# The last batch's first product as eight groups of seven block products, in another order of the tail

## The chip, the cores and the metric

The kernel runs on one core of a Trainium2 chip. The metric is the device time of one execution in microseconds (us); a kernel's time is the median of its runs. Of each kernel one execution was recorded by the hardware profiler; its engines are PE (TensorE, the matrix unit, whose results land in PSUM banks), DVE (VectorE), ACT (ScalarE), POOL (GpSimd) and SP (which issues DMAs).

## What is computed

Attention with normalised queries and keys, and behind it two matrix products with an activation between:

```python
q_n = q / (norm(q) + 1e-6);  k_n = k / (norm(k) + 1e-6)          # 8 batches, 12 heads, 448 x 64
attn = softmax(q_n @ k_n.T / tau);  x = (attn @ v)               # as 3584 tokens x 768
h = x @ w_in                                                     # 768 x 2048, the first product
g = h * clip(h + 3, 0, 6) / 6                                    # "hardswish"
out = g @ w_out                                                  # 2048 x 768, the second product
```

## The kernel before

**Stages.** A batch has 448 tokens and six pairs of heads. A plan written out by hand starts the kernel; then a loop takes one pair of heads after the other, and puts between the attention's steps matmul *units* of the two products of earlier batches. After the last pair, the *tail* has the units that are left: a part of the first product of batch 6, the whole first product of batch 7, and the second products of batches 5 to 7. The change lies in the tail alone, some 60 us.

**The order of the tail** is written out by hand in `LAST` (line 62), and read by `listed` (line 1034) into a list of units, `units[NP]` (lines 1109 to 1113). `do("UU", len(stream), "avp")` (line 1279) issues one unit after the other. A unit issues its matmuls and hangs steps that finish it on three lists, for ACT, DVE and POOL; after each unit the three lists are emptied in that order, and a step may hang a further step on a list. So the text of `LAST` sets the order of every engine's queue, and each engine works its queue strictly in order.

**Banks.** Six PSUM banks (four named M, and Y and Z) are taken in turn (`next_bank`, line 166) by whatever unit asks for a new one. A unit can start only when the last reader of what its bank held before is done.

**The first product, plain.** `mm1_unit` (line 581) makes 128 of the 2048 features for 448 tokens: 6 matmuls of 448 columns (L587), a relu on ACT (L596), and a product with a clip on DVE (L602). In the list these are `f14` (batch 6) and `F6` (batch 7).

**The first product, in seven block products.** `seven_unit` (line 920) makes two such units, n and n + 8, at once: both matrices are cut in 2 x 2 blocks, and seven products of sums of blocks (Strassen's way, Winograd's form of the numbers 1 to 7) give the four blocks of the result, with 3 matmuls of 224 columns for each, 21 in all (L947). A group is issued in four parts: `A2` is products 3 and 4 of group 2, `B2` is product 7, `C2` products 5 and 2, `D2` product 6; product 1 goes with A or B. The parts A and C share one bank, B and D another. The finishing steps of a group:

- after A, ACT copies the first results to SBUF (L1001, L1003), and POOL adds their halves (L1006). The letter of `M1_BY` says how product 1 gets in: with `p`, product 1 is issued with A and POOL adds it (L1008); with `v`, it is issued with B and DVE adds it later.
- after C, ACT makes the relu (L970) of two of the four result blocks, DVE makes the differences for the other two (L1014, or L1017 and L1019 where the letter is `v`) and the product with the clip for the first two (L973).
- after D, DVE makes the last sum (L1022); then ACT makes its relu (L984) and the clip and product follow. The letter of `H_BY` says where: `v` is DVE (L992), `p` is POOL.

The scratch for these (`trio`) has room for three groups. The seven products need sums of blocks of the weights (`w_sum_of`, L898, in the list `w7.2v`: product 7, groups 4 and 5, on DVE; part p serves groups 2p and 2p + 1) and of the activations (`x_sum_of`, L915, in the list `x4`). Before the change, groups 0 to 5 are made this way, and units 6, 7, 14 and 15 are plain.

**The second product** takes pairs of 128-token blocks, numbered 0 to 10, in the same seven products: `4.7` (`product_unit`, line 769, 8 matmuls of 384 columns, L788) is product 4 of pair 7. Pairs 9 and 10 are those of batch 7, so they need all sixteen units of the first product; product 4 reads the odd rows of g, product 3 the even ones. `g9:6` is the sum of blocks for product 6 of pair 9 (`g_sum`, L766). Products 3, 4, 5 and 2 are copied out by ACT (L836, L807), 1, 6 and 7 are added by DVE (L845, L813), and POOL makes three sums of a pair's parts (L817, L818, L821). `s6.1` (`single_unit`, line 859, 16 matmuls, L868) is a 128-token block of batch 6 that has no partner, and DVE copies it out (L878). `gl` copies a left-over part of g between batches (L578).

Of the kernel before, what the change touches and what calls it, by code (L numbers as in the profile page):

```python
# [59 lines left out]
]  # L60

LAST = [
# [3 lines left out]
]  # L66
H_BY, M1_BY = "vvvvvvpp", "pppvpppp"


@with_exitstack  # L70
def kernel(
# [543 lines left out]
    def result(b, t, cols, o, end=None):  # L615
        for e in range(2):
            if t < 3:
                r = out[b * S : (b + 1) * S].rearrange("(p c) m -> c p m", c=7)[2 * t + e + b % 2]
            else:
                r = out[(b - 1 + e) * S : (b + e) * S].rearrange("(p c) m -> c p m", c=7)[6 * (1 - e)]  # L620
            eng = nc.scalar if end is not None and e else nc.sync
            eng.dma_start(out=r[:, cols], in_=o[64 * e : 64 * e + 64, 0 : cols.stop - cols.start])
# [146 lines left out]
    def product_unit(n, name, end=None, apart=False):  # L769

        need = {"3": ["y3"], "4": ["y4"], "1": "1", "6": "6", "7": "7"}.get(name, [])
        assert all((x, c) in summed for x in need for c in range(KC))
        if name not in "34":
            assert (n, name) in g_summed
        base = None if apart else {"2": "4", "5": "3", "6": "1"}.get(name)
        if base is None:
            banks[n, name] = bank_of(None, 1)
        ps, key = banks.pop((n, base)) if base else banks[n, name]
        c0, width = (MH // 2 * end, MH // 2) if end in (0, 1) else (0, MH)
        if name in "167":  # L780
            lhs, rhs = sum_of(n, name), w_sum[name]
        else:
            i, k = {"3": (0, 0), "4": (1, 1), "2": (1, 0), "5": (0, 1)}[name]
            m = LEFT if name in "42" else RIGHT
            lhs, rhs = block(n, i, k), w_out_sb[:, :, m].rearrange("p (c k) m -> p c k m", k=2)[:, :, k, :]
        m = ps[:, c0 : c0 + width]
        for c in range(KC):
            nc.tensor.matmul(  # L788
                m,
                lhs[:, c, :],  # L790
                rhs[:, c, c0 : c0 + width],
                start=(base is None and c == 0),
                stop=(c == KC - 1),
                skip_group_check=True,
            )
        issued_products.add((n, name))
        d, e = d_and_e(n)
        if base is None and name in "34":
            unread[key] = 1 + ((n, name) not in APART)

        def done(i, o, cols):
            unread[key] = 0
            result(*PAIRS[n][i], cols, o, end)

        def copied(i, cols):
            o = out_tile()
            nc.scalar.copy(out=o[:, :], in_=m)  # L807
            parts[n, name] = o
            done(i, o, cols)

        def added(i, cols, x):
            parts[n, name] = o = out_tile()
            nc.vector.tensor_tensor(out=o[:, 0:width], in0=m, in1=x[:, c0 : c0 + width], op=ALU.add)  # L813
            done(i, o, slice(cols.start + c0, cols.start + c0 + width))

        def both():
            nc.gpsimd.tensor_tensor(out=e, in0=d, in1=e, op=ALU.add)  # L817
            nc.gpsimd.tensor_tensor(out=d, in0=e, in1=parts[n, "5"][:, :], op=ALU.subtract)  # L818

        def rest():  # L820
            nc.gpsimd.tensor_tensor(out=e, in0=e, in1=parts[n, "2"][:, :], op=ALU.subtract)  # L821

        def added_later(i, cols, x):
            parts[n, name] = o = out_tile()
            nc.scalar.copy(out=o[:, :], in_=m)
            unread[key] = 0

            def add():
                nc.gpsimd.tensor_tensor(out=o[:, :], in0=o[:, :], in1=x, op=ALU.add)
                result(*PAIRS[n][i], cols, o)  # L830

            post["p"].append(add)

        def finish():
            if name in "34":
                nc.scalar.copy(out={"3": d, "4": e}[name], in_=m)  # L836
                unread[key] -= 1
            elif apart:
                added_later(*{"5": (0, RIGHT, d), "2": (1, LEFT, e)}[name])
            elif name == "5":  # L840
                copied(0, RIGHT)
            elif name == "2":
                copied(1, LEFT)
            elif name == "1":
                nc.vector.tensor_tensor(out=d, in0=m, in1=d, op=ALU.add)  # L845
            elif name == "6":
                added(1, RIGHT, e)
            else:
                added(0, LEFT, d)
            ready.add((n, name))  # L850
            first = {(n, x) for x in ("245" if (n, "4") in APART else "45")}
            if (n, name) in first and first <= ready:
                post["p"].append(both)
            if name in "245" and {(n, "4"), (n, "5"), (n, "2")} <= ready:
                post["p"].append(rest)

        post["a" if name in "2345" else "v"].append(finish)

    def single_unit(b, m):

# [59 lines left out]
    def seven_unit(n, part):  # L920
# [39 lines left out]
        def g_out(first):  # L960
# [4 lines left out]
            step = (FCN // 2 * (S + SR) + (-HS if first else HS)) // 2  # L965
            return bass.AP(tensor=g.tensor, offset=g.offset, ap=[g.ap[0], [step, 2], [1, HS // 2]]).bitcast(BF16)

        def relu():
            u = sb.tile([128, S], BF16, name="u", tag="u", bufs=3)
            nc.scalar.activation(out=u[:, :], in_=ps[:, 0:S], func=AF.Relu, bias=half_bias, scale=1.0 / 6.0)  # L970

            def product():
                nc.vector.scalar_tensor_tensor(  # L973
                    out=g_out(1), in0=halves_of(u[:, :]), scalar=1.0, in1=halves_of(ps[:, 0:S]), op0=ALU.min, op1=ALU.mult
                )
                unread[key] = 0

            post["v"].append(product)

        def clipped():  # L980
            u = sb.tile([128, S], BF16, name="u", tag="u", bufs=3)
            e = H_BY[n]
            if e == "v":
                nc.scalar.activation(out=u[:, :], in_=h, func=AF.Relu, bias=half_bias, scale=1.0 / 6.0)  # L984
            else:
                nc.scalar.activation(out=s, in_=h, func=AF.Relu, bias=half_bias, scale=-1.0 / 6.0)
                nc.scalar.activation(out=u[:, :], in_=s, func=AF.Relu, bias=1.0, scale=-1.0)

            def product():
                o, x, y = g_out(0), halves_of(u[:, :]), halves_of(h)  # L990
                if e == "v":
                    nc.vector.scalar_tensor_tensor(out=o, in0=x, scalar=1.0, in1=y, op0=ALU.min, op1=ALU.mult)  # L992
                else:
                    nc.gpsimd.tensor_tensor(out=o, in0=x, in1=y, op=ALU.mult)
                g_done.update(((BL, n), (BL, n + FCN // 2)))
                seven_done.add(n)

            post[e].append(product)
# [11 lines left out]
            post["p"].append(added)  # L1010

        def differences():
            if M1_BY[n] == "p":
                nc.vector.tensor_tensor(out=h, in0=t, in1=ps[:, 0:S], op=ALU.subtract)  # L1014
                return
            same = t[:, HS:S].unsqueeze(1).to_broadcast([128, 2, HS])
            nc.vector.tensor_tensor(out=halves_of(h), in0=same, in1=halves_of(ps[:, 0:S]), op=ALU.subtract)  # L1017
            m1 = seven[n]["B"][0][:, HS:S]
            nc.vector.tensor_tensor(out=h[:, 0:HS], in0=m1, in1=h[:, 0:HS], op=ALU.add)  # L1019
# [40 lines left out]
    def products(text):  # L1060

        u = []
        for x in text.split():
            name, n = x.split(".")
            if name[0] == "s":
                u.append((single_unit, int(name[1]), int(n)))
            else:
                u.append((product_unit, int(n), name[0], None, name[1:] == "a"))
        return u
# [37 lines left out]

    assert len(carry) == 2
    units[NP] = [x for line in LAST for x in listed(line)]
    units[NP] += products("3.9 4.9") + sums(9, "1") + products("5.9") + sums(10, "75") + products("2.9 3.10") + sums(10, "62")  # L1110
    units[NP] += products("4.10 5.10") + sums(10, "1") + products("2.10 1.9 1.10")
    units[NP] += [(product_unit, n, x, 2) for n, x in ((9, "7"), (9, "6"), (10, "6"))]
    units[NP] += [(product_unit, 10, "7", x) for x in range(2)]

# [200 lines left out]
```

## Time and profile before

| | us |
|---|---|
| runs | 403.27, 403.36, 404.13 (median 403.36) |
| the profiled execution's own time | 403.54 |
| its span, first to last instruction | 401.7 |
| TensorE busy | 392.0 |
| tail: 4.7 starts | 339.1 |
| tail: the first group starts | 349.2 |
| tail: the first product of pairs 9 and 10 starts | 379.4 |

A row of the profile's timeline reads: start and length in us, engine, line, operation, what is written from what is read, partitions x elements and types, count; in brackets, how long the engine stood idle before and whom it waited for. Matmul lengths overlap, so the price of a piece is the step from its start to the next one's. PEld is the loading of weights into TensorE. The chain is the row of work that ended last, followed back. A tile's name is that of its memory: `at`, `nrm`, `tT`, `xT` and `gT` are reused in the tail, so that `big<-w_in_sb` or `nrm<-w_in_sb` is a weight sum, `at<-xT` a sum of activations, and `gT<-...` with f32 the scratch of a group.

### The profile page before, as it was taken

How to read it: one execution, taken by the hardware profiler on the slowest of the kernel's cores; microseconds unless marked ns; L12 is line 12 of the kernel's file. 1: busy time of each engine (PE TensorE's matmuls, PEld its weight loads, DVE VectorE, ACT ScalarE, POOL GpSimd, SP SyncE). 2: the span in 40 equal slices, each digit the busy share in tenths (PEclk: the TensorE clock that was granted, in tenths of full speed). 3: DMA queues.
4: the chain of work that ended last, by engine and by line, in shares of the span. 5: the costliest groups of instructions: out<-in, count | busy, mean ns of one | idle time of the engine just before them, and what ended most of it. 6: DMA issues, size and time to landing. Idle time of an engine off the chain costs nothing.

```text
span 401.7 us, 9814 instructions
## 1 busy us (share of the span) xinstructions
PE 392.0 (98%) x3743; PEld 239.4 (60%) x3743; DVE 300.9 (75%) x535; ACT 280.2 (70%) x615; POOL 262.8 (65%) x253
## 2 busy tenths in 40 slices
PE   7988999999999999999999999999999999999996
PEld 5656556555665556655555556556555556687563
DVE  7998787877588777777857887587656676888863
ACT  5999989887377687787768768768758755265330
POOL 6899936753644996598486875776674893344270
PEclk9999999999999999999999999999999999999999
DMA  8999999698868658686779748966763522130133
GB/s 288 317 237 227 200 226 250 137 202 191 194 156 200 146 115 223 172 214 137 182 192 203 166 117 164 180 187 140 187 154 80 111 47 55 34 79 21 39 81 97
DMA packets 93166, 63.75 MB, mean 159 GB/s; under 512 B 56128, under 2 KB 93120, under 8 KB 93120
## 3 DMA queue, kind: packets, MB, share of 16 engines
q1 hardware_dynamic: 87408, 56.45, 59.6%
q0 software_dynamic: 5312, 6.29, 9.6%
q8 instruction: 29, 0.48, 0.5%
q10 hardware_dynamic: 400, 0.39, 0.3%
q14 instruction: 17, 0.14, 0.1%
HBM read 45.61 MB, written 11.01 MB: 141 GB/s over the span
## 4 chain that ended last, share of the span: by engine, by line
PE 91%; ACT 4%; DVE 4%; issue 1%; ACTq 0%; DVEq 0%
PE M L587 21%; PE M L788 16%; PE PV L482 11%; PE Z L587 6%; PE M L442 6%; PE Y L587 5%; PE Z L788 5%; PE Y L788 5%; PE M L868 4%; PE M L634 3%; ACT at L460 2%; PE PV L1136 2%; PE M L947 2%; PE Y L442 1%; PE Z L442 1%; DVE n L248 1%
## 5 line engine op out<-in xcount | busy, mean ns | idle before, releaser
L460 ACT ACTIVATE at<-M 128x448 bf16<-128x448 f32 x194 | 96.6, 562 | 23.2 <-PE M L442 20.6
L587 PE MATMUL M<-xT,w_in_sb 128*128 128x448 bf16 x462 | 99.2, 352 | 0.2
L587 PEld LDWEIGHTS <-w_in_sb 128*128 128x128 bf16 x696 | 65.3, 98 | 56.8 <-issue 2.8
L293 POOL TENSOR_TENSOR nrm<-big,r 128x896 bf16<-128x896 f32 (+1 forms) x47 | 78.7, 1679 | 15.4 <-issue 5.5
L236 POOL TENSOR_TENSOR big<-big 128x896 f32<-128x896 f32 (+5 forms) x45 | 68.5, 1528 | 12.9 <-DVE gT L602 8.3
L482 PEld LDWEIGHTS <-at 128*128 128x128 bf16 (+1 forms) x1536 | 54.1, 97 | 19.9 <-issue 12.1
L602 DVE SCALAR_TENSOR_TENSOR gT<-u,M 128x448 bf16<-128x448 bf16 x73 | 44.6, 618 | 28.5 <-ACT u L596 27.8
L482 PE MATMUL PV<-vx,at 128*128 128x65 bf16 (+1 forms) x1536 | 62.7, 193 | 0.0
L596 ACT ACTIVATE u<-M,bias 128x448 bf16<-128x448 f32 x77 | 50.2, 656 | 15.1 <-PE M L587 14.7
L399 POOL COPY km<-tT 64x128 bf16<-64x128 bf16 x34 | 14.4, 423 | 60.8 <-DMA tT<-nrm 26.3
L248 DVE TENSOR_REDUCE n<-big 128x14 f32<-128x896 f32 (+1 forms) x50 | 51.6, 1038 | 0.3 <-ACT big L234 0.2
L788 PEld LDWEIGHTS <-gT 128*128 128x128 bf16 x288 | 27.8, 98 | 19.0 <-DVE gT L766 0.2
L788 PE MATMUL M<-w_out_sb,gT 128*128 128x384 bf16 x192 | 35.0, 326 | 0.0
L503 DVE TENSOR_TENSOR on<-PV,rc 128x512 bf16<-128x512 f32 x48 | 33.2, 692 | 1.7
L442 PE MATMUL M<-tT,kz 64*128 64x448 bf16 (+1 forms) x171 | 30.9, 351 | 0.5 <-ACT at L460 0.5
L460 ACT ACTIVATE at<-Y 128x448 bf16<-128x448 f32 x50 | 28.1, 562 | 4.3 <-PE Z L442 4.3
L788 PEld LDWEIGHTS <-gs 128*128 128x128 bf16 x224 | 21.5, 98 | 14.7 <-DVE gs L766 0.4
L312 POOL CAST vx<-big 128x512 bf16<-128x512 f32 x39 | 28.3, 730 | 2.9 <-DMA big<-in_v_dram 2.8
L460 ACT ACTIVATE at<-Z 128x448 bf16<-128x448 f32 x50 | 28.1, 563 | 2.6 <-PE M L442 2.6
L587 PE MATMUL Z<-xT,w_in_sb 128*128 128x448 bf16 x120 | 26.0, 353 | 0.0
L587 PE MATMUL Y<-xT,w_in_sb 128*128 128x448 bf16 x114 | 24.7, 352 | 0.0
L766 DVE TENSOR_TENSOR gs<-gT 128x1024 bf16<-128x1024 bf16 x26 | 23.5, 904 | 0.0
(165 smaller groups left out, 641.4 us busy)
## 6 DMA issues: line engine op xcount, KB each, us to landing
big<-in_k_dram SPq DMA_DIRECT2D x24, 448.0 KB, 4.9
big<-in_q_dram SPq DMA_DIRECT2D x24, 448.0 KB, 4.3
out_dram<-o SPq DMA_DIRECT2D x107, 96.0 KB, 2.2
big<-in_v_dram SPq DMA_DIRECT2D x48, 128.0 KB, 4.6
big<-in_v_dram SPq DMA_DIRECT2D x48, 96.0 KB, 4.5
w_in_sb<-in_moe_w_in_dram POOLq DMA_DIRECT2D x8, 384.0 KB, 9.1
w_out_sb<-in_moe_w_out_dram POOLq DMA_DIRECT2D x4, 768.0 KB, 10.6
tT<-nrm SPq DMA_TRANSPOSE x34, 2.8
```

Source lines behind the costliest of these rows:

```text
L236: engines[e].tensor_tensor(out=o, in0=i, in1=i, op=ALU.mult)
L248: nc.vector.tensor_reduce(out=n2_and_r[0][:, d % 2, j % 2, c], in_=sq[:, :, :, :].rearrange("p g c d -> p (g c) d")[:, c, :], axis=AX.X, o ...
L293: engines[e].tensor_tensor(out=nrm[:, :, g, :].rearrange("p c g d -> p g c d"), in0=raw_of[j][:, g, :, :], in1=n2_and_r[4][:, d % 2, j % 2, :]
L312: (engines[e].copy if e == "a" else engines[e].tensor_copy)(out=o, in_=f)
L442: nc.tensor.matmul(o, ks, qt[rows], start=True, stop=True)
L460: nc.scalar.activation(out=o, in_=x, func=AF.Exp, scale=inv_tau)
L482: nc.tensor.matmul(pv_out(j, h), at[rows, n, q_cols(i // HP, j)], vt[rows, 3 + h if name == "M" else 5 * h + int(name[1]), :], start=(name ...
L503: nc.vector.tensor_tensor(out=on[:, :, :, :].rearrange("p j h d -> p h j d"), in0=pv4[:, :, :, 0:D], in1=rc[:, :, :].to_broadcast([128, 2, ...
L587: nc.tensor.matmul(ps[:, 0:S], w_in_sb[:, cc, fc * 128 : (fc + 1) * 128], x[:, cc, 0:S], start=(cc == 0), stop=(cc == CC - 1),)
L596: nc.scalar.activation(out=u[:, :], in_=ps[:, 0:S], func=AF.Relu, bias=half_bias, scale=1.0 / 6.0)
L602: nc.vector.scalar_tensor_tensor(out=g[:, fc, c0 : c0 + S], in0=u[:, :], scalar=1.0, in1=ps[:, 0:S], op0=ALU.min, op1=ALU.mult,)
L788: nc.tensor.matmul(m, lhs[:, c, :], rhs[:, c, c0 : c0 + width], start=(base is None and c == 0), stop=(c == KC - 1), skip_group_check=True,)
```

## The change

Groups 6 and 7 are made as seven block products too, in the place of the plain units F6, F7, F14 and F15; all twelve weight sums that are left stand in the tail's list (seven before). The order of the tail is another one, written out to the end; the letters for the groups are others; and POOL gets more: the clip product of groups 1, 2 and 3 (`H_BY`), the first clip product of groups 6 and 7 (the new `C_BY`: ACT copies the bank and makes both relus, `clip_later`, and POOL multiplies), and the sum of product 7.8 (the new `BY_POOL`: ACT copies, POOL adds). In before no `H_BY` letter of a group that is made is `p`. The two relus of a POOL clip use the scratch `t` in place of `s`.

```diff
 LAST = [
-    "w1.2v g7:1 w5.2p 4.7 f14 f15 2.7 x4 x1 g6:e x3 x6 w7.2v g8:6 x7 g8:7 1.7 7.7 g8:5 s6.1 A0 6.7 w2.1v g8:2",
-    "4.8 B0 A1 w6.2v w7.1v A3 C0 C1 B1 2.8 D0 D1 F15 B3 w2.2p C3 A2 F7 B2 D3 C2 A5 D2 s6.0 gl C5 A4 g8:1 3.8",
-    "B4 B5 C4 D4 D5 5.8 F14 F6 1.8 g9:6 g9:7 7.8 6.8 g9:5 g9:2",
+    "g7:1 w7.1v w2.2p 4.7 f14 x1 x3 x4 f15 2.7 1.7 g8:7 w1.3v A0 3.8 x7 g8:6 x6 6.7 g8:5 B0 w2.1v C0 A1 5.8",
+    "D0 w1.2v w7.2v B1 C1 A2 A3 D1 g8:1 B2 g8:2 C2 4.8 7.7 B3 C3 A5 D2 w5.2v w6.2v 2.8 B5 w5.3v D3 1.8 C5 A4",
+    "6.8 D5 w2.3v w7.3v A7 B4 w6.3v C4 A6 C7 B7 g6:e D7 C6 B6 gl D6 D4 7.8 s6.1 s6.0 g10:6 4.10 g10:7 g9:7",
+    "g10:5 4.9 g9:5 3.9 g9:6 3.10 5.9 g10:2 g10:1 2.10 g9:2 5.10 g9:1 1.9 1.10 2.9",
 ]
-H_BY, M1_BY = "vvvvvvpp", "pppvpppp"
+H_BY, M1_BY, C_BY = "vpppvvvv", "vpvvvvpp", "vvvvvvpp"
+BY_POOL = "7.8".split()
...
+        def by_pool():
+            if name != "1":
+                added_later(*{"6": (1, RIGHT, e), "7": (0, LEFT, d)}[name])
+                return
...
+        def clip_later():
+            u = sb.tile([128, S], BF16, name="u", tag="u", bufs=3)
+            nc.scalar.activation(out=t, in_=ps[:, 0:S], func=AF.Relu, bias=half_bias, scale=-1.0 / 6.0)
+            unread[key] = 0
+            nc.scalar.activation(out=u[:, :], in_=t, func=AF.Relu, bias=1.0, scale=-1.0)
+            post["p"].append(
+                lambda: nc.gpsimd.tensor_tensor(out=g_out(1), in0=halves_of(u[:, :]), in1=halves_of(s), op=ALU.mult)
+            )
+
         def relu():
+            if C_BY[n] == "p":
+                nc.scalar.copy(out=s, in_=ps[:, 0:S])
+                return
...
         def differences():
+            if C_BY[n] == "p":
+                post["a"].append(clip_later)
...
-    units[NP] += products("3.9 4.9") + sums(9, "1") + products("5.9") + sums(10, "75") + products("2.9 3.10") + sums(10, "62")
-    units[NP] += products("4.10 5.10") + sums(10, "1") + products("2.10 1.9 1.10")
```

In the changed kernel's lines, POOL's multiplications are L1018 (groups 1 to 3) and L986 (6 and 7), its half sums L1030 and L1032, DVE's weight sums L910, its clip products L1016, its last sums L1048, and the groups' matmuls L959. The end of the list is as before: 7.9, 6.9, 6.10 and product 7.10 in two halves.

More of the change, by code (lines that the diff above doesn't have):

```diff
@@ L829, in add @@
                 nc.gpsimd.tensor_tensor(out=o[:, :], in0=o[:, :], in1=x, op=ALU.add)
-                result(*PAIRS[n][i], cols, o)
+                result(*PAIRS[n][i], cols, o, end)
             post["p"].append(add)
+        def by_pool():
+            if name != "1":
+                added_later(*{"6": (1, RIGHT, e), "7": (0, LEFT, d)}[name])
+                return
+            o = out_tile()
+            nc.scalar.copy(out=o[:, :], in_=m)
+            post["p"].append(lambda: nc.gpsimd.tensor_tensor(out=d, in0=o[:, :], in1=d, op=ALU.add))
         def finish():
@@ L843, in finish @@
                 copied(1, LEFT)
+            elif f"{name}.{n}" in BY_POOL:
+                by_pool()
             elif name == "1":
@@ L855, in finish @@
                 post["p"].append(rest)
-        post["a" if name in "2345" else "v"].append(finish)
+        post["a" if name in "2345" or f"{name}.{n}" in BY_POOL else "v"].append(finish)
     def single_unit(b, m):
@@ L985, in clipped @@
             else:
-                nc.scalar.activation(out=s, in_=h, func=AF.Relu, bias=half_bias, scale=-1.0 / 6.0)
-                nc.scalar.activation(out=u[:, :], in_=s, func=AF.Relu, bias=1.0, scale=-1.0)
+                nc.scalar.activation(out=t, in_=h, func=AF.Relu, bias=half_bias, scale=-1.0 / 6.0)
+                nc.scalar.activation(out=u[:, :], in_=t, func=AF.Relu, bias=1.0, scale=-1.0)
             def product():
```

## The prediction

> **What bounds the kernel now.** I read the page's busy shares and its chain first, then the tail by stages, then TensorE's own timeline in the tail.
>
> ```profile
> PE 392.0 (98%) x3743; PEld 239.4 (60%) x3743; DVE 300.9 (75%) x535; ACT 280.2 (70%) x615; POOL 262.8 (65%) x253
> PE 91%; ACT 4%; DVE 4%; issue 1%; ACTq 0%; DVEq 0%
> ```
>
> TensorE is busy 98% of the span and carries 91% of the chain. The other engines matter where they hold TensorE up. The stages of the tail (columns: length, then busy time of PE, PEld, DVE, ACT, POOL) say how near they come:
>
> ```profile
> 349.16:364.24 15.08, 15.08 (x131) 12.43 (x129) 12.60 (x24) 8.06 (x17) 6.53 (x8) 1.00 0.25 54
> 364.24:379.41 15.17, 14.91 (x104) 9.80 (x103) 12.70 (x22) 7.22 (x15) 6.32 (x7) 1.00 0.13 27
> ```
>
> PE is full at clock 1.00, DVE has some 2.5 us free in each 15, ACT about half, POOL more than half. Now TensorE's timeline (start, length, instructions):
>
> ```profile
> 339.09 1.46 PE L788 MATMUL M<-w_out_sb,gT 128*128 128x384 bf16 x8
> 340.39 1.30 PE L587 MATMUL M<-xT,w_in_sb 128*128 128x448 bf16 x6
> 341.52 1.30 PE L587 MATMUL Y<-xT,w_in_sb 128*128 128x448 bf16 x6
> 346.56 1.46 PE L868 MATMUL M<-w_out_sb,gT 128*128 128x384 bf16 x8
> 347.86 1.46 PE L868 MATMUL M<-w_out_sb,big 128*128 128x384 bf16 x8
> 349.16 0.74 PE L947 MATMUL M<-at,w_in_sb 128*128 128x224 bf16 x6
> 349.73 0.45 PE L947 MATMUL M<-at,big 128*128 128x224 bf16 x3
> 350.02 1.46 PE L788 MATMUL Z<-w_sum,gs 128*128 128x384 bf16 x8
> 368.33 1.46 PE L788 MATMUL M<-w_out_sb,gT 128*128 128x384 bf16 x8
> 369.96 0.45 PE L947 MATMUL Z<-at,big 128*128 128x224 bf16 x3 [0.16 <-ACT gT L1003]
> 372.98 2.69 PE L587 MATMUL M<-xT,w_in_sb 128*128 128x448 bf16 x12
> 375.51 1.46 PE L788 MATMUL M<-w_sum,big 128*128 128x384 bf16 x8
> 379.41 1.46 PE L788 MATMUL Z<-w_out_sb,big 128*128 128x384 bf16 x8
> 395.01 1.46 PE L788 MATMUL Y<-w_sum,gs 128*128 128x384 bf16 x8
> ```
>
> Lengths overlap; the price of a piece is the step from start to start. Six matmuls of 448 columns step 340.39 to 341.52, 1.135 us; three or six of 224 columns 0.29 and 0.57, 0.0957 each; a product of eight 1.30; a single of sixteen 346.56 to 349.16, 2.60.
>
> **The change, part by part.** Both kernels issue the same up to the product 4.7 at 339.09, and the same fourteen products of pairs 9 and 10 at the end, the first at 379.41 now. What changes is the 40.32 us between.
>
> *TensorE's work.* Before: 12 products 15.60, two singles 5.20, six plain units (f14, f15, F6, F7, F14, F15) 6.81, six groups of 21 matmuls at 2.01, 12.06: together 39.67. So 0.65 us of the 40.32 is standing still. The rows show it: the product at 368.33 should end at 369.63 and the next piece starts 0.33 later, after an ACT copy; twelve matmuls at 372.98 take 2.53 instead of 2.27, 0.26 lost to a bank that two DVE sums free, as the chain of waits has it:
>
> ```profile
> 373.17 1.16 DVE gT L1022 x2
> ```
>
> After: 15.60 + 5.20 + f14 and f15 2.27 + eight groups 16.08 = 39.15. Four plain units (4.54) leave and two groups (4.02) come: 0.52 saved. If nothing stands still any more the gain is 40.32 - 39.15 = 1.17 us. What the new order stands still is the whole question; call it S.
>
> *Who must be ready.* I laid the new order end to end from 339.09 and for each piece looked up what frees its bank (six, taken in turn) and what makes its operands. Prices of the helpers, DVE first, then POOL, then ACT (start, length):
>
> ```profile
> 348.64 0.68 DVE L766 TENSOR_TENSOR big<-gT 128x1024 bf16<-128x1024 bf16 x1
> 349.24 0.55 DVE L845 TENSOR_TENSOR big<-Z,big 128x384 f32<-128x384 f32 x1
> 353.23 1.01 DVE L898 TENSOR_TENSOR big<-w_in_sb 128x768 bf16<-128x768 bf16 x2
> 361.11 0.62 DVE L1017 TENSOR_TENSOR gT<-gT,M 128x448 f32<-128x448 f32 x1
> 361.77 0.39 DVE L1019 TENSOR_TENSOR gT<-M,gT 128x224 f32<-128x224 f32 x1
> 362.07 0.61 DVE L973 SCALAR_TENSOR_TENSOR big<-u,M 128x448 bf16<-128x448 bf16 x1
> 365.88 1.00 DVE L992 SCALAR_TENSOR_TENSOR big<-u,gT 128x448 bf16<-128x448 bf16 x1
> 366.81 0.61 DVE L973 SCALAR_TENSOR_TENSOR big<-u,Y 128x448 bf16<-128x448 bf16 x1
> 367.34 0.61 DVE L1022 TENSOR_TENSOR gT<-Z,gT 128x448 f32<-128x448 f32 x1
> 367.88 0.54 DVE L878 COPY o<-M 128x384 f32<-128x384 f32 x1
> 368.75 0.63 DVE L992 SCALAR_TENSOR_TENSOR big<-u,gT 128x448 bf16<-128x448 bf16 x1 [0.33 <-ACT u L984]
> 396.56 0.56 DVE L813 TENSOR_TENSOR o<-Y,big 128x384 f32<-128x384 f32 x1 [0.74 <-PE Y L788]
> ```
> ```profile
> 356.26 1.64 POOL L898 TENSOR_TENSOR big<-w_in_sb 128x768 bf16<-128x768 bf16 x1
> 365.75 0.66 POOL L1006 TENSOR_TENSOR gT<-gT 128x224 f32<-128x224 f32 x1 [2.84 <-ACT gT L1001]
> 366.48 0.92 POOL L1008 TENSOR_TENSOR gT<-gT 128x224 f32<-128x224 f32 x1
> 387.96 0.99 POOL L817 TENSOR_TENSOR big<-big 128x384 f32<-128x384 f32 x1 [0.94 <-ACT big L836]
> ```
> ```profile
> 365.15 0.52 ACT L1001 COPY gT<-M 128x448 f32<-128x448 f32 x1
> 368.05 0.67 ACT L984 ACTIVATE u<-gT,bias 128x448 bf16<-128x448 f32 x1 [2.13 <-DVE gT L1022]
> 368.62 0.61 ACT L970 ACTIVATE u<-M,bias 128x448 bf16<-128x448 f32 x1
> 369.83 0.48 ACT L836 COPY big<-M 128x384 f32<-128x384 f32 x1
> ```
>
> DVE's steps: 448 columns 0.54, a block sum 0.60, a weight sum 0.5, the pair L1017 and L1019 0.66 and 0.30, a 384 sum 0.48. DVE gains six weight sums (3.0), four more groups that finish without GpSimd's half (4 x 0.42, since 0.66 and 0.30 replace 0.54), two more groups (difference, sum, clip: 3.2), and loses four plain products (2.2), the clips of groups 1 to 3 (1.6) and product 7.8's sum (0.5): +3.6 against some 5 us free. On average it fits; it must fit at each place.
>
> POOL's new multiplication (448 columns, bf16 by f32, five times) stands in no row. It lies between the 224 sum, 0.66, and the 768 bf16 sum, 1.64; I take 0.99 x 448/384 = 1.15, by the row nearest in size. ACT's two passes for it are bounded by 0.48 (a 384 copy) and 0.67 (L984); I take 0.57, the step 368.05 to 368.62. The Trainium skill (GPSIMD Engine Reference, section 3.1) has 2.6 cycles per element for two inputs at 1.2 GHz, which is an estimate of 0.97 us here, and its section 4.1 speaks against the move: an elementwise multiplication belongs on VectorE, GpSimd being about twice as slow. By its price the sum below would not change; the trace agrees with the factor (384 columns in 0.99 on POOL, 0.55 on DVE). These multiplications and product 7.8's move (ACT 0.48, POOL 0.99) are covered by 7.8, s6.1 and s6.0, 6.5 us between the last group and product 4.10; without that cover they would cost their length.
>
> *The port.* DVE's 365.88 row takes 1.00 where the same instruction takes 0.63 at 368.75. POOL's 365.75 sum ends at 366.41, and DVE ends 0.47 later; POOL's next, at 366.48, ends at 367.40, 0.52 after DVE. So a DVE instruction with both inputs in SBUF and a POOL instruction run one after the other, in the order of their asking; the L1022 row, with an input in PSUM, is not slowed.
>
> *Where it is close.* (1) A5 is wanted by TensorE at 359.2 in the bank of C2. Group 0's last sum starts at 352.3, its clip 0.71 + 0.70 later (L1022 to L984 to L992), at 353.7; then in DVE's queue clip 0.54, w7.2 0.55, three of group 1 1.62, two block sums 1.20, 0.66, 0.30, and C2's product 0.61: 359.2. Level: 0 to 0.2, I take 0.1. (2) B7 and D7 are wanted at 369.73 and 370.02 and need w7.3 and w6.3, which stand last in DVE's queue behind group 5's clip. Product 6.8 starts at 364.70; DVE reads it 1.55 after its start (395.01 to 396.56), at 366.25; group 5's last sum at 366.73, its relu 367.44, its clip 368.14 to 368.77. ACT then copies A7 (368.01 to 368.53), and POOL asks for its 224 sum at 368.6, as the clip runs. POOL ends at 369.29 (+0.52), w7.3 at 369.76 (+0.47), POOL's second sum at 370.28, w6.3 at 370.75. D7 starts 0.73 late. (3) After D4, DVE, ACT and POOL finish groups 7, 6 and 4 by about 378.6 on the same walk, 4.10 is wanted at 379.1 and reads only odd rows (group 7); 3.9, which needs groups 6 and 4, is 2.6 later. No cost. The remaining releases have 0.2 us or more to spare.
>
> S = 0.1 + 0.73, so 1.17 - 0.83 = 0.34 gained: 403.54 - 0.34 = 403.2 against the profiled execution's 403.54. The runs' median, 403.36, is 0.18 below that; on its scale the forecast is **403.0**.
>
> **Rivals.** *A, nothing stands still:* DVE's w7.3 and w6.3 go ahead of POOL's two sums, or DVE is 0.5 us earlier there. Against it: the port rows above. For it: the two engines meet within 0.1 us. 403.36 - 1.17 = 402.2. *B*, the forecast, 403.0 (402.6 to 404.1 as the port's turns fall). *C, slower: GpSimd's multiplication is dearer.* At 2.0 us each, those of groups 1 and 2 with the two sums of pair 8 between them hold the port to 364.5; w5.3, asked for at 362.6, ends at 364.95, C5's product at 367.5 (0.54, 0.48, 0.66, 0.30, 0.61 behind it), B4 waits 0.4; the third multiplication and its followers then push w6.3 to 372.3. S = 2.3, 403.36 - 1.17 + 2.3 = 404.5. S is 0.8 at 1.15 us and 2.3 at 2.0: it decides from 1.35 us, where S passes 1.17, and shows from 1.8. For it: only sizes that differ are in the trace; against it: 768 columns take 1.64. *D, the change saves no matmul time:* 224-column matmuls would have to slow down among 384-column ones; 349.73 to 350.02 shows they do not.
>
> **How the numbers follow.** A 0.30, B 0.47, C 0.16, and 0.07 for a wait that none of these has, 0.03 of it faster and 0.04 slower. A measurement can tell 0.2% (0.8 us) from no change: faster by more 0.33, within 0.47, slower 0.20. The range reaches from A with 0.1 below to C with 0.2 above: 402.1 to 404.7.
>
> **What would show it.** In TensorE's timeline after: 21 matmuls of 224 for each of eight groups, products 4.7 to the first of pair 9 or 10 in 39.15 + S. Step (2) shows as a wait of D7's weights on DVE L910, 0.5 to 0.9 long, with POOL's L1030 and L1032 beside stretched L910 rows; A would have no wait there; C would show POOL L1018 at 1.5 or more and waits at B4. A wait in the products of pairs 9 and 10 would make step (3) wrong, and a bank wait over 0.3 in the first ten microseconds the walk as a whole.

## The result, and the profile after

| | before | after |
|---|---|---|
| median of the runs | 403.35 (6 runs, 402.95 to 404.13) | 406.73 (6 runs, 406.61 to 407.51) |
| ratio after to before | | 1.0085 (95% interval 1.0072 to 1.0098) |
| span of the profiled execution | 401.7 | 404.8 |
| tail: from the last pair's first value matmul (32 of 65 columns) to the last product's first half | 58.29 | 61.71 |

The changed kernel is 3.4 us slower, outside the forecast's range, and all of it lies in the tail: 61.71 - 58.29 = 3.42. A ratio below can differ from that of two medians. Single runs of one kernel scatter by half a microsecond, in the largest set (35 runs of before) by 3.9, and the tail's length repeats to 0.01 where the same kernel was profiled twice, so the experiments are read by the tail and by the waits in it.

The page of the changed kernel: TensorE's busy time is the same, its share of the chain fell from 91% to 82%, and DVE's rose from 4% to 9%.

```profile
PE 392.2 (97%) x3761; PEld 240.7 (59%) x3761; DVE 303.8 (75%) x543; ACT 284.5 (70%) x623; POOL 266.1 (66%) x258
PE 82%; DVE 9%; ACT 5%; issue 2%; POOL 1%; DVEq 0%; ACTq 0%; POOLq 0%
```

The two stages of its tail, from 4.7 to 4.10 and from 4.10 on (length; busy PE, PEld, DVE, ACT, POOL). PE now has 2.0 and 1.2 us without work, where the same view of before's tail has 0.26 in all:

```profile
338.77:380.80 42.03, 40.01 (x314) 29.57 (x311) 34.33 (x64) 21.03 (x41) 19.17 (x22) 1.00 0.17 36
380.80:400.88 20.08, 18.88 (x120) 11.18 (x119) 13.69 (x20) 4.93 (x11) 8.28 (x7) 1.00 0.39 89
```

TensorE's timeline of the changed kernel, the pieces that stood still; in brackets the idle time beyond the pipelined end of the piece before, and the releaser:

```profile
338.77 1.46 PE L790 MATMUL M<-w_out_sb,gT 128*128 128x384 bf16 x8
358.63 0.45 PE L959 MATMUL M<-xT,big 128*128 128x224 bf16 x3
359.68 0.75 PE L959 MATMUL Z<-at,w_in_sb 128*128 128x224 bf16 x6 [0.60 <-DVE big L997]
365.16 1.46 PE L790 MATMUL M<-w_sum,big 128*128 128x384 bf16 x8
367.08 0.45 PE L959 MATMUL M<-at,big 128*128 128x224 bf16 x3 [0.45 <-DVE gT L1045]
370.52 0.45 PE L959 MATMUL M<-xT,tT 128*128 128x224 bf16 x3
370.96 0.46 PE L959 MATMUL Y<-at,tT 128*128 128x224 bf16 x3
371.90 0.46 PE L959 MATMUL Y<-at,tT 128*128 128x224 bf16 x3 [0.47 <-DVE tT L910]
378.83 1.46 PE L880 MATMUL Y<-w_out_sb,gT 128*128 128x384 bf16 x8
380.80 1.46 PE L790 MATMUL Z<-w_out_sb,big 128*128 128x384 bf16 x8 [0.51 <-DVE gT L1048]
382.10 5.57 PE L790 MATMUL M<-w_out_sb,big 128*128 128x384 bf16 x32
388.20 1.47 PE L790 MATMUL Z<-w_out_sb,big 128*128 128x384 bf16 x8 [0.53 <-DVE big L768]
389.51 1.46 PE L790 MATMUL M<-w_out_sb,big 128*128 128x384 bf16 x8
391.61 1.47 PE L790 MATMUL M<-w_sum,big 128*128 128x384 bf16 x8 [0.64 <-DVE big L768]
```

Step by step against the prices of the prediction (0.0957 for a matmul of 224 columns, 1.30 for a product): A5 comes 0.76 late (359.68 where 358.92 was due), D5, the three matmuls at 367.08, 0.62, B7 0.15, D7 0.65, 4.10 0.67, 2.10 0.90, 1.9 0.80. Together 4.55. Before had 0.65. The difference, 3.90, less 0.52 of matmuls saved, is 3.38.

### The profile page after: what moved, and what is told of

Its sections match the earlier page's. It is cut to its first block, busy times and chain, and to the rows that moved or that the text cites. A ratio compares the mean times of both kernels' runs of the same rounds, so it can differ in the third digit from the quotient of the medians.

```text
span 404.8 us, 9865 instructions
## 1 busy us (share of the span) xinstructions
PE 392.2 (97%) x3761; PEld 240.7 (59%) x3761; DVE 303.8 (75%) x543; ACT 284.5 (70%) x623; POOL 266.1 (66%) x258
## 4 chain that ended last, share of the span: by engine, by line
PE 82%; DVE 9%; ACT 5%; issue 2%; POOL 1%; DVEq 0%; ACTq 0%; POOLq 0%
PE M L589 20%; PE M L790 13%; PE PV L484 11%; PE Z L589 6%; PE M L444 6%; PE Y L589 5%; PE Z L790 4%; PE Y L790 4%; PE M L636 3%; PE M L880 3%; ACT at L462 2%; PE PV L1160 2%; DVE big L768 2%; PE Y L444 1%; PE Z L444 1%
## 5 line engine op out<-in xcount | busy, mean ns | idle before, releaser
L589 PEld LDWEIGHTS <-w_in_sb 128*128 128x128 bf16 x672 | 62.9, 98 | 54.7 <-issue 2.5
L589 PE MATMUL M<-xT,w_in_sb 128*128 128x448 bf16 x438 | 94.0, 352 | 0.1
L598 ACT ACTIVATE u<-M,bias 128x448 bf16<-128x448 f32 x73 | 47.9, 658 | 14.5 <-PE M L589 14.1
L790 PE MATMUL M<-w_out_sb,gT 128*128 128x384 bf16 x208 | 37.9, 326 | 0.0
```

The source lines that it names most:

```text
L589: nc.tensor.matmul(ps[:, 0:S], w_in_sb[:, cc, fc * 128 : (fc + 1) * 128], x[:, cc, 0:S], start=(cc == 0), stop=(cc == CC - 1),)
L790: nc.tensor.matmul(m, lhs[:, c, :], rhs[:, c, c0 : c0 + width], start=(base is None and c == 0), stop=(c == KC - 1), skip_group_check=True,)
```

## The experiments

Four theories. **Q**: what costs is which instruction stands in front of which in an in-order queue. **P**: the port that DVE and GpSimd share; **D**: DVE simply has too much to do; **G**: clips on GpSimd cost by themselves. The rows that the theories start from, in the changed kernel's DVE, ACT and POOL timelines:

```profile
356.56 0.69 DVE L768 TENSOR_TENSOR gT<-gT 128x1024 bf16<-128x1024 bf16 x1
358.05 0.62 DVE L1043 TENSOR_TENSOR gT<-gT,Z 128x448 f32<-128x448 f32 x1 [0.80 <-ACT u L994]
358.70 0.39 DVE L1045 TENSOR_TENSOR gT<-M,gT 128x224 f32<-128x224 f32 x1
359.01 0.61 DVE L997 SCALAR_TENSOR_TENSOR big<-u,Z 128x448 bf16<-128x448 bf16 x1
...
365.98 0.62 DVE L1043 TENSOR_TENSOR gT<-gT,Z 128x448 f32<-128x448 f32 x1 [1.13 <-ACT u L994]
...
369.35 0.63 DVE L1016 SCALAR_TENSOR_TENSOR big<-u,gT 128x448 bf16<-128x448 bf16 x1 [0.33 <-ACT u L1008]
369.89 1.95 DVE L910 TENSOR_TENSOR tT<-w_in_sb 128x768 bf16<-128x768 bf16 x2
...
376.22 0.62 DVE L1040 TENSOR_TENSOR gT<-gT,M 128x448 f32<-128x448 f32 x1 [1.22 <-ACT gT L991]
...
379.26 0.43 DVE L580 COPY big<-gT 128x1024 bf16<-128x1024 bf16 x1 [1.89 <-POOL big L986]
...
380.13 0.61 DVE L1048 TENSOR_TENSOR gT<-Z,gT 128x448 f32<-128x448 f32 x1
...
382.58 0.55 DVE L890 COPY o<-Y 128x384 f32<-128x384 f32 x1
383.04 1.28 DVE L768 TENSOR_TENSOR gs<-big 128x1024 bf16<-128x1024 bf16 x2
384.25 3.90 DVE L768 TENSOR_TENSOR big<-big 128x1024 bf16<-128x1024 bf16 x5
...
388.67 2.88 DVE L768 TENSOR_TENSOR big<-big 128x1024 bf16<-128x1024 bf16 x2
```
```profile
356.14 0.67 ACT L1010 ACTIVATE gT<-gT,bias 128x448 f32<-128x448 f32 x1 [1.46 <-DVE gT L1048]
356.84 0.58 ACT L1011 ACTIVATE u<-gT 128x448 bf16<-128x448 f32 x1
357.32 0.62 ACT L994 ACTIVATE u<-Z,bias 128x448 bf16<-128x448 f32 x1
...
364.08 0.67 ACT L1010 ACTIVATE gT<-gT,bias 128x448 f32<-128x448 f32 x1 [0.17 <-DVE gT L1048]
364.78 0.58 ACT L1011 ACTIVATE u<-gT 128x448 bf16<-128x448 f32 x1
365.26 0.61 ACT L994 ACTIVATE u<-Z,bias 128x448 bf16<-128x448 f32 x1
```
```profile
357.50 1.04 POOL L1018 TENSOR_TENSOR big<-u,gT 128x448 bf16<-128x448 bf16 x1 [1.89 <-ACT u L1011]
...
369.81 0.68 POOL L1030 TENSOR_TENSOR gT<-gT 128x224 f32<-128x224 f32 x1 [2.59 <-ACT gT L1025]
370.57 0.86 POOL L1032 TENSOR_TENSOR gT<-gT 128x224 f32<-128x224 f32 x1
371.38 0.98 POOL L1030 TENSOR_TENSOR gT<-gT 128x224 f32<-128x224 f32 x1
...
378.19 1.03 POOL L986 TENSOR_TENSOR big<-u,gT 128x448 bf16<-128x448 bf16 x1 [1.94 <-ACT u L984]
...
385.45 1.54 POOL L819 TENSOR_TENSOR big<-big 128x384 f32<-128x384 f32 x1 [2.40 <-ACT big L846]
388.32 1.28 POOL L820 TENSOR_TENSOR big<-big,o 128x384 f32<-128x384 f32 x1 [1.33 <-ACT o L809]
```

What they say. DVE's differences of C2 (358.05) stood idle for ACT's relu of C2. Both only read the bank of C2, and the program makes the one wait for the other. That relu (357.32) stood behind the two passes of group 1's clip, of which the first waited for DVE's last sum of group 1. The Trainium skill (PSUM — Partial Sum Buffer, section "PSUM bank collisions raise a hardware error") states a rule that fits: the compiler's scheduler adds a dependency between any two instructions of different engines that touch the same partitions of one bank, reads and writes alike, ACT against DVE too. The trace agrees: the first difference of each group begins only after the end of its relu (of ACT's copy in groups 6 and 7).

Product 4.10 takes the bank Z after D4, so it starts when group 4's last sum (380.13) has read that bank; this sum stands in DVE's queue behind `gl` (379.26), which stood idle 1.89.

Before had the wait of one reader for the other already. ACT's relu of a bank (L970) stood behind a relu (L984) that waited for DVE's last sum of another group, and DVE's difference of the same bank (L1014) stood idle 1.39, though TensorE's last matmuls into the bank began at 362.80 and took 0.45:

```profile
364.06 0.67 ACT L984 ACTIVATE u<-gT,bias 128x448 bf16<-128x448 f32 x1 [1.28 <-DVE gT L1022]
364.63 0.61 ACT L970 ACTIVATE u<-Y,bias 128x448 bf16<-128x448 f32 x1
```
```profile
365.35 0.62 DVE L1014 TENSOR_TENSOR gT<-gT,Y 128x448 f32<-128x448 f32 x1 [1.39 <-ACT u L970]
```

Each wait, in us, by kernel (the two expectations that speak of B4's wait of 0.62 mean D5's: the three matmuls at 367.08 are D5, not B4):

| | tail | A5 | D5 | B7 and D7 | 4.10 | 2.10 | 1.9 | others |
|---|---|---|---|---|---|---|---|---|
| after | 61.71 | 0.76 | 0.62 | 0.80 | 0.67 | 0.90 | 0.80 | |
| e1_clip_after_relu | 60.91 | 0 | 0.16 | 0.79 | 0.68 | 0.89 | 0.81 | B5 0.40 |
| e2_gl_late | 60.90 | 0.75 | 0.62 | 0.79 | 0 | 0.76 | 0.80 | |
| e3_w_early | 61.02 | 0.77 | 0.62 | 0 | 0.35 | 0.90 | 0.80 | B0 0.32, D0 0.11 |
| e4_c_v | 61.08 | 0.76 | 0.62 | 0.79 | 0 | 0.91 | 0.80 | |
| e5_all_v | 61.18 | 0.70 | 0.67 | 0.79 | 0 | 0 | 0 | 6.8 1.16, 5.9 0.64 |
| e6_s_act | 61.63 | 0.78 | 0.62 | 0.80 | 0.69 | 0.78 | 0.80 | |
| e7_no_pool_sums | 60.24 | 0.78 | 0.62 | 0.80 | 0.68 | 0.21 | 0 | |
| e8_best_v, e12_best_v_again | 57.45 | 0 | 0.16 | 0 | 0 | 0 | 0 | B5 0.12 |
| e9_best_p | 58.02 | 0 | 0.16 | 0 | 0 | 0.20 | 0 | B5 0.11, s6.1 0.37 |
| e10_best_hv | 59.92 | 0 | 0 | 0 | 0 | 0 | 0 | D3 0.67, B5 0.25, 6.8 1.66, s6.1 0.13 |
| e11_six_groups | 57.94 | 0 | 0.16 | none made | 0 | 0 | 0 | B5 0.12 |

### e1_clip_after_relu

```diff
-            post["a"].append(clipped)
+            (held if n in (1, 3) else post["a"]).append(clipped)
...
             nc.scalar.activation(out=u[:, :], in_=ps[:, 0:S], func=AF.Relu, bias=half_bias, scale=1.0 / 6.0)
+            post["a"].extend(held)
+            held.clear()
```

> The changed kernel with one edit in the order of ACT: the two relus for GpSimd's clips of groups 1 and 3 are issued behind the next group's first relu instead of ahead of it; no work is added, taken or moved to another engine. Theory Q (queues: what costs is which instruction stands in front of which in an in-order queue): DVE's differences of C2 and C5 wait for the relu of the same bank on ACT, and that relu stands behind two passes that wait for DVE; so A5's wait (0.76 us late) falls to 0.1 or less and B4's (0.62) to 0: 1.2 us faster than the changed kernel, some 405.5. Rival P (the port that DVE and GpSimd share): GpSimd does the same work, so 0.2 at most. Rival D (DVE simply has too much to do): no change.

405.99 us, tail 0.80 shorter than after. Nothing but ACT's order changed, and A5's wait went; D5's fell to 0.16. ACT's relu of C2, then DVE's differences, in this kernel:

```profile
355.19 0.63 ACT L995 ACTIVATE u<-Z,bias 128x448 bf16<-128x448 f32 x1 [0.74 <-PE Z L960]
```
```profile
356.95 0.61 DVE L1046 TENSOR_TENSOR gT<-gT,Z 128x448 f32<-128x448 f32 x1
```

The relu comes two microseconds earlier, and DVE goes on behind its block sums without a gap. Q holds; P expected 0.2 at most, D nothing. 0.4 of the 1.2 came back as a wait of B5: TensorE, no longer held at A5, reaches B5 before DVE has done C3.

### e2_gl_late

```diff
-... B7 g6:e D7 C6 B6 gl D6 D4 7.8 ...
+... B7 g6:e D7 C6 B6 D6 D4 gl 7.8 ...
```

> The changed kernel with gl moved from behind B6 to behind D4, nothing else. Theory Q: gl waits in DVE's queue for GpSimd's multiplication of group 6 (1.89 us idle before it) and holds up the last sums of groups 6 and 4 behind it; moved behind them, the wait of 0.67 before 4.10 goes and the sums for pairs 9 and 10 begin about 1.2 us earlier, so that the two waits on them (0.9 and 0.8) shrink: 1.0 to 1.5 us faster, 405.2 to 405.7. Rival P: the multiplication still holds the port, and the waits on the sums come from the port: 0.3 at most. Rival D: DVE has the same work, no change.

406.36 us, tail 0.81 shorter. 4.10's wait went, so Q is right that gl, which waited 1.89 for GpSimd's multiplication, held up the last sums. The two waits on the block sums stayed (0.76, 0.80): the sums began 2.1 us after 4.10 (382.14 and 380.03) where it had been 2.2. That part of Q's expectation failed.

### e3_w_early

```diff
-... f15 2.7 1.7 ...  B2 g8:2 C2 ...  D5 w2.3v w7.3v A7 B4 w6.3v C4
+... f15 2.7 w7.3v 1.7 ...  B2 g8:2 w6.3v C2 ...  D5 w2.3v A7 B4 C4
```

> The changed kernel with the weight sums w7.3 and w6.3 moved from behind group 5's clip to two places where DVE stood idle (ahead of 1.7's sum, and ahead of C2's differences). Step 2 of the prediction (they meet GpSimd's sums of A7 on the shared port, and D7 waits): D7's and B7's waits, 0.15 and 0.65, go: 0.7 to 0.8 us faster, 406.0. Rival D: DVE has the same work, no change. If the early place of w6.3 meets GpSimd's multiplication of group 1, A5's wait grows by up to 0.3 and the gain falls to 0.5.

405.99 us, tail 0.69 shorter. B7's and D7's waits went, as step (2) had it; 4.10's halved. A new one of 0.32 appeared at B0, which needs x7: w7.3, put ahead of 1.7's result, took 1.18 beside GpSimd's last sum of pair 7, w1.3 then took 1.01 beside GpSimd's sum of A0, and x7 stands behind both.

### e4_c_v

```diff
-H_BY, M1_BY, C_BY = "vpppvvvv", "vpvvvvpp", "vvvvvvpp"
+H_BY, M1_BY, C_BY = "vpppvvvv", "vpvvvvpp", "vvvvvvvv"
```

> The changed kernel with the first clip products of groups 6 and 7 back on DVE (the C_BY letters all v): GpSimd loses two multiplications, ACT four passes, DVE gains two instructions of 0.54. Theory Q: gl no longer waits for GpSimd, DVE no longer waits for ACT's copies of C6 and C7; 4.10's wait of 0.67 goes and the sums for pairs 9 and 10 begin some 2 us earlier, so the waits of 0.9 and 0.8 mostly go: 1.8 to 2.2 us faster, 404.7. Rival D (DVE is the bound at the end): 1.1 us more on DVE, 0.5 to 1.1 us slower, 407.5.

406.00 us, tail 0.63 shorter: a third of what Q expected and not the loss that D expected. 4.10's wait went, the waits on the sums did not. DVE now had two clips more, stood idle 1.39 for ACT's relu of C6's bank, and came to the sums 2.25 us after 4.10 (385.16 and 382.91), no sooner than in the changed kernel.

### e5_all_v

```diff
-H_BY, M1_BY, C_BY = "vpppvvvv", "vpvvvvpp", "vvvvvvpp"
-BY_POOL = "7.8".split()
+H_BY, M1_BY, C_BY = "vvvvvvvv", "vpvvvvpp", "vvvvvvvv"
+BY_POOL = []
```

> The changed kernel's order with all of GpSimd's new work given back: all clips on DVE (H_BY and C_BY all v), product 7.8 added by DVE. Theory Q (it is the order in the queues): group 1's clip on DVE stands ahead of the second block sum and waits for ACT, so A5's wait stays at 0.5 to 0.8; B4's stays above 0.3; D7's stays; 4.10's goes, the waits on the sums of pairs 9 and 10 stay, since DVE has 3 us more to do: 405.5 to 406.7. Rival G (the clips on GpSimd are what costs): the time falls below 403.4.

407.13 us, tail 0.53 shorter than after and 2.9 longer than before. G falls: with none of the new work on GpSimd the new order is about as slow. A5's wait is 0.70, now behind group 1's clip on DVE, and product 6.8 waits 1.16 for DVE's sum of 1.8, on whose bank it adds. The waits of 2.10 and 1.9 are gone although the ten sums begin 2.7 us after 4.10 (385.19 and 382.50): they take 6.1 us, and GpSimd's first sum, asked for among them, ends only 0.85 after the last of them, at 392.14:

```profile
386.39 3.10 DVE L768 TENSOR_TENSOR big<-big 128x1024 bf16<-128x1024 bf16 x5
```
```profile
387.15 4.99 POOL L819 TENSOR_TENSOR big<-big 128x384 f32<-128x384 f32 x1 [11.74 <-ACT big L846]
```

Why GpSimd got no turn here, where it got one in the changed kernel, stays open.

### e6_s_act

```diff
-        post["v"].append(store)
+        post["a" if b == BL - 1 else "v"].append(store)
```

with `nc.scalar.copy` for batch 6 in the step itself.

> The changed kernel with the copies of the two singles s6.1 and s6.0 on ACT in place of DVE, nothing else. Theory Q: the ten sums for pairs 9 and 10 stand behind those copies in DVE's queue and begin 0.9 us earlier; 2.10's wait of 0.9 goes, and 1.9's of 0.8 comes down to what the total lateness was, 1.7 less 0.9: 0.8 us faster than the changed kernel, 405.9. Rival P (the waits on the sums come from the port, on which they meet GpSimd's sums of the parts): the sums are stretched as before, 0 to 0.4 faster.

406.82 us, tail 0.08 shorter: Q's 0.8 did not come. The first two sums, on DVE, and product 7.8's sum on POOL:

```profile
383.01 1.97 DVE L768 TENSOR_TENSOR gs<-big 128x1024 bf16<-128x1024 bf16 x2
```
```profile
382.76 1.07 POOL L831 TENSOR_TENSOR o<-o,big 128x384 f32<-128x384 f32 x1 [2.76 <-ACT o L827]
```

They began 0.8 us sooner after 4.10 and then took 1.97 instead of 1.28, as they met GpSimd on the port; the rest was stretched as before. P is right here.

### e7_no_pool_sums

```diff
-            if (n, name) in first and first <= ready:
+            if n < 9 and (n, name) in first and first <= ready:
...
-            if name in "245" and {(n, "4"), (n, "5"), (n, "2")} <= ready:
+            if n < 9 and name in "245" and {(n, "4"), (n, "5"), (n, "2")} <= ready:
```

> The changed kernel without GpSimd's three sums of the parts for pairs 9 and 10 (six instructions left out, so that the outputs of these pairs lack them). Rival P: DVE's ten sums then take 6.2 us instead of 8.7, the waits of 2.10 and 1.9 go, 1.7 us faster than the changed kernel, 405.0. Theory Q: the sums still begin 2.2 us after 4.10, the eighth ends 7.0 us after 4.10 and 2.10 is wanted 6.5 after it: 2.10's wait falls from 0.9 to 0.5, 1.9's goes: 1.2 us faster, 405.5.

This kernel leaves out GpSimd's sums of the parts of pairs 9 and 10. 405.10 us, tail 1.47 shorter. DVE's sums without GpSimd beside them:

```profile
384.21 3.09 DVE L768 TENSOR_TENSOR big<-big 128x1024 bf16<-128x1024 bf16 x5
...
387.82 1.29 DVE L768 TENSOR_TENSOR big<-big 128x1024 bf16<-128x1024 bf16 x2
```

All ten took 6.1 us (383.00 to 389.11) where after took 8.5 (383.04 to 391.55). Of the two waits, 1.70, 0.21 was left. So at this place it is the port, P, on top of a late start.

### e8_best_v and e12_best_v_again

The changed kernel with e1's edit, e6's, C_BY all v, and this order:

```diff
-g7:1 w7.1v w2.2p 4.7 ...  4.8 7.7 B3 C3 A5 D2 w5.2v w6.2v 2.8 B5 w5.3v D3 1.8 C5 A4
+g7:1 w7.1v w7.3v w2.2p 4.7 ...  4.8 7.7 B3 w6.3v C3 A5 D2 w5.2v w6.2v 2.8 w5.3v D3 B5 1.8 C5 A4
-6.8 D5 w2.3v w7.3v A7 B4 w6.3v C4 A6 C7 B7 g6:e D7 C6 B6 gl D6 D4 7.8 ...
+6.8 D5 w2.3v A7 B4 C4 A6 C7 gl B7 C6 g6:e D7 B6 D6 D4 7.8 ...
```

> Eight groups with every wait found so far mended by order alone: GpSimd's clips of groups 1 and 3 behind the next first relu on ACT; w7.3 beside w7.1 at the start and w6.3 ahead of C3; D3 ahead of B5; C6 ahead of D7; gl ahead of B7; the singles' copies on ACT; the first clips of groups 6 and 7 on DVE. Theory Q: TensorE's waits between 4.7 and the end fall from 4.6 to 0.4 us or less, and the matmuls saved show: 402.3 to 402.8, faster than the kernel before (403.4). Rival D (eight groups give DVE more than it can do in this time): waits of 1.2 or more stay, 403.6 or slower.

> The same kernel as e8_best_v, for its distance from the kernel before and from the three beside it on one chip: 0.8 to 1.1 us faster than before, 0.998 to 0.997.

402.27 us beside 403.25 for before (ratio 0.9986, 0.9968 to 1.0004), and once more 402.77 beside 403.58 (0.9974, 0.9952 to 0.9996). The first interval reaches past 1, so the gain rests on the second and on the tail. The tail is 57.45 both times, 0.84 shorter than before, 4.26 shorter than after. From 4.7 to 4.10 TensorE has no idle time that the view shows:

```profile
338.57:378.06 39.49, 39.49 (x315) 29.63 (x312) 36.22 (x68) 20.02 (x39) 17.00 (x20) 1.00 0.18 39
```

39.49 is the prediction's 39.15 and 0.34 of small waits. D falls: DVE is busy 36.2 of 39.5 and keeps up when nothing stands in front of what is due. The ten sums take 8.4 us here too, beside GpSimd's (378.59 to 386.99), but begin 0.5 us after 4.10 (378.06) and not 2.2: with an early start the port costs TensorE nothing.

### e9_best_p, e10_best_hv and e11_six_groups

```diff
# e9_best_p, e10_best_hv: letters against e8_best_v
-H_BY, M1_BY, C_BY = "vpppvvvv", "vpvvvvpp", "vvvvvvvv"
+H_BY, M1_BY, C_BY = "vpppvvvv", "vpvvvvpp", "vvvvvvpp"
+H_BY, M1_BY, C_BY = "vvvvvvvv", "vpvvvvpp", "vvvvvvvv"
# e11_six_groups: order against e8_best_v, and without w1.3 w2.3 w5.3 w6.3 w7.3
-6.8 D5 w2.3v A7 B4 C4 A6 C7 gl B7 C6 g6:e D7 B6 D6 D4 7.8
+6.8 D5 F7 B4 C4 F15 gl F6 g6:e F14 D4 7.8
```

> The mended order (e8_best_v) with the first clips of groups 6 and 7 on GpSimd again, as the change has them. Theory Q: gl now stands ahead of those multiplications and C6 ahead of D7, so nothing of DVE waits behind them; DVE has 1.1 us less, ACT four passes more: within 0.3 us of e8_best_v. Rival G (clips on GpSimd cost by themselves, through the port or their length): 0.7 us or more slower than e8_best_v.

403.54 us, tail 0.57 longer than e8_best_v's: more than Q's 0.3, near G's 0.7. The larger wait, 0.37 in s6.1, is a queue's again: DVE's block sum for s6.1 stands behind the differences of C6, which stood idle 1.46 for ACT's copy of that bank. The other, 0.20 at 2.10, was not followed up.

> The mended order (e8_best_v) with the clips of groups 1, 2 and 3 on DVE, so that GpSimd has none of the five multiplications. DVE gains three instructions of 0.54. In e8_best_v DVE runs without a gap from group 0's clip to product 7.7's sum, where A5 follows with nothing to spare, so theory D (a full DVE queue) expects A5 0.4 to 0.6 us late, 0.5 to 1.0 us slower in all; rival G: 0.3 us or more faster, since the port is free.

405.03 us, tail 2.47 longer: G is wrong in sign, D in size and place. A5 is on time; group 1's clip, 1.16 long, meets a sum of GpSimd's and pushes what is behind it. Group 1's clip, and the place on TensorE:

```profile
358.47 1.16 DVE L1022 SCALAR_TENSOR_TENSOR big<-u,gT 128x448 bf16<-128x448 bf16 x1
```
```profile
366.80 1.46 PE L790 MATMUL M<-w_sum,big 128*128 128x384 bf16 x8 [1.49 <-DVE big L857]
```

6.8 waited for DVE's sum of 1.8, which stood behind group 2's clip, two weight sums and a last sum. So in this order the clips of groups 1 to 3 belong on GpSimd.

> The mended order (e8_best_v) with groups 6 and 7 as the plain units F6, F7, F14 and F15, and without the five weight sums that only they need: 24 matmuls of 448 columns in place of 42 of 224. If the two groups are worth their matmuls, TensorE's pieces from 4.7 to 4.10 are 0.5 us longer and the kernel 0.5 us slower than e8_best_v, 402.8. Rival (the gain of e8_best_v is its order, and the two groups give back on DVE what they save): the same as e8_best_v or up to 0.3 faster.

403.68 us, tail 0.49 longer than e8_best_v's, with the same waits. The two groups are worth their matmuls, 0.52 by the prediction, once nothing waits for them.

## Why the prediction was wrong

- **TensorE's work** held. 39.15 and the waits, 2.85, give the 42.0 us from 4.7 to 4.10; e11_six_groups against e12_best_v_again measures the saving, 0.49 for 0.52. S was the whole question, as the text said; it was 4.55 and not 0.83: 2.85 before 4.10 and 1.70 behind it.
- **Step (1), A5 "level: 0 to 0.2"**, is the first that failed: 0.76. The sum of DVE's steps was right (in e1_clip_after_relu it leaves no wait), but it let DVE's differences start when DVE was free. They wait for ACT's relu of the same bank, and the relu stood behind the clip's two passes. The rows of before showed it: DVE's L1014 stood idle 1.39 for ACT's L970. The same failure a few pieces on made most of D5's 0.62 (0.46 of it went in e1_clip_after_relu), at a place that the step "the remaining releases have 0.2 us or more to spare" covered.
- **Step (2), D7 "0.73 late"**, held in size and cause: 0.80 with B7, DVE's two weight sums stretched to 1.95 between POOL's sums, gone in e3_w_early.
- **Step (3), "no cost"**, failed most: 0.67 + 0.90 + 0.80. The walk let DVE run through; in fact it stood 1.22 for ACT's copy of C6's bank (the mechanism of step 1) and 1.89 at gl, which waits for GpSimd's multiplication of group 6 though by the code the two write different columns. 4.10 itself waited for the bank that group 4's last sum, behind gl, had to free. And the walk ended at 4.10: the ten block sums behind it began 2.2 us after it and took 8.5 us, where 6.1 are enough without GpSimd's sums of the parts (e7_no_pool_sums). Either cure is nearly enough: without those sums 0.21 of the 1.70 is left, with an early start nothing (e8_best_v).
- **Rival C** had the sign and not the mechanism. The multiplication took 1.04, less than the 1.15 of the sum. The price of the Trainium skill (GPSIMD Engine Reference, section 3.1), as the prediction worked it out, was an estimate of 0.97. The advice of its section 4.1, to keep such work on VectorE, was wrong in the order of e8_best_v for groups 1 to 3 (e10_best_hv, 2.47 longer on DVE) and right for 6 and 7 (e9_best_p, 0.57 longer on GpSimd).
- **The chances** gave 0.07 to "a wait that none of these has". Four such waits, at D5, 4.10, 2.10 and 1.9, make 2.99 of the 4.55. The walk had not followed DVE's queue behind 4.10 at all, and the range should have been wider upward for that.

Left open: what the first products after 4.10 would take in another order of the ten sums, which was not tried; why gl is made to wait, which was read from the code and moved, not taken apart; and what decides whether GpSimd gets a turn between two of DVE's sums.

## What to carry to other kernels

When an order of in-order queues is checked by hand, look at every instruction's releasers in the trace, not only at those that the data asks for: two engines that read one PSUM bank waited for each other here, and then an instruction parked in front on either engine holds both. Walk on until the last dependent piece, past the point where the main engine seems safe. A change that saves 0.5 us of matmuls was worth having only after eight places had been mended (six of the order, two of the engine), each by moving something forward, back or to another engine, none by taking work away.

## What the runs showed of the hardware

- DVE's block sums, with both inputs in SBUF, and GpSimd's sums do not run side by side: ten block sums took 8.5 us beside GpSimd's work and 6.1 without it, and GpSimd's 384-column sum took 1.54 instead of 1.00. The Trainium skill (SBUF — State Buffer, section "SBUF: two separate sides") calls it an exclusive lock for the whole instruction; the traces agree. Who comes next differs: in the changed kernel the waiting side got the next turn (DVE's two weight sums in 1.95 between GpSimd's), in e5_all_v GpSimd's sum stood behind six more of DVE's (4.99 long).
- GpSimd's product of a bf16 and an f32 operand of 448 columns took 1.04 us, hardly more than its f32 sum of 384 (0.99 to 1.00): the mixed types cost nothing that shows.
- The waits repeat from kernel to kernel to 0.02 us (D7's is 0.64 or 0.65 in seven kernels, 1.9's 0.80 or 0.81 in six), while whole runs scatter by far more.
